# Decay attention and max-MoE on one core: scores of a head as one unit on four lent PSUM banks, and the decays' clip first

## The chip, the cores and the metric

The kernel runs on one core of a Trainium2 chip. The core's engines work side by side, each through its own queue in order: PE (matrix multiply, with PEld for its weight loads), DVE, ACT and POOL (elementwise work and reductions) and SP, which issues the DMAs here. The metric is device time of one execution in microseconds (us), less is better. A measurement of this kernel is the median of a few runs.

## The reference

Decay attention over 8 batches of 8 heads with 576 queries, then a layer of three matrices with a maximum, and an output matrix. All is fp32.

```python
# q, k, v: (8, 8, 576, 64); f: (8, 8, 576); w1, w2, w3: (512, 768); w_out: (768, 512)
scores = scale * np.matmul(q, k.transpose(0, 1, 3, 2))
log_f = np.log(np.clip(f, 0.0001, 1.0))
cum = np.cumsum(log_f, axis=-1)
decay = cum[:, :, :, None] - cum[:, :, None, :]
scores = np.where(causal, -1000000000.0, scores + decay)     # causal: above the diagonal
scores = scores - np.max(scores, axis=-1, keepdims=True)
attn = np.exp(scores)
attn = attn / (np.sum(attn, axis=-1, keepdims=True) + 1e-09)
x = heads side by side of np.matmul(attn, v)                 # (4608, 512)
h = np.maximum(np.maximum(x @ w1, x @ w2), x @ w3)
out = h @ w_out
```

## The kernel before

**Stages.** Heads are numbered n = 0 to 63, eight to a batch. The first batch (n < 8) has a form of its own: q and k come by DMA, PE turns them (`turn_head`, L551), ACT and DVE copy the turned halves out of PSUM (L560, L562), and the matmuls take fp32 operands. From the second batch on (56 heads) scores are made in two passes of faster fp32r matmuls. Pass A (L742) makes the scores with the decay in them. The mask is then added on the diagonal blocks, by PE for n < 16 (L758) and by DVE after that (`cover` L779, `cover_last` L784). ACT and DVE take the maximum over the key blocks (L817, L805, L807, L810), POOL reduces it over the partitions (L820), POOL casts it into a row of the query operand (L823), and pass B (L742 again) adds a term with the negative maximum to the same PSUM columns. ACT takes the exponential out of PSUM (L841). From n = 16 on the sums of the exponentials are made by DVE (L850, L854, L857) and POOL (L865). The values of two heads are multiplied together (`values_pair`, L911), and each batch's result goes through the MoE: `gemm1` (L1071, three matrices) and `gemm2` (L1102, output matrix). The last batch has its own form of the MoE (`moe_last`, L1267).

**Units and banks.** Scores are transposed: keys on the 128 partitions, queries along the columns, five key blocks (the last one 64 keys wide), and only the part on or below the diagonal. A head from the second batch on is two units: unit 2 holds queries 0 to 255 (two matmuls in each pass, of 256 and 128 columns, in bank `sp2`), unit 1 queries 256 to 575 (five matmuls: 320, 320, 192 and 64 columns as one run in banks `sp1/1` and `sp1/0`, and 320 columns as a second run in `sp1/2`). So these four of the eight PSUM banks belong to the scores, and the other four (`mp0` to `mp2`, `t0`) form a pool: a step of `gemm1`, `gemm2` or `values_pair` names a `Slot` in `take=`, gets the bank that came free first, and the step that empties the bank names it in `drop=`. `plan.lend` puts a bank into that pool, the scores' four only at the end, for `moe_last`.

**What sets the order.** Every function only adds steps to `Plan` (engine, cost, keys read and written, priority). `Plan.emit` then lists the steps by a model of the engines: each engine takes, of its steps that are ready, the one with the lowest rank. The rank is the priority, less a share of the length of the chain behind the step, plus a shift drawn at random from `SEEDS` for each four units of priority. Each engine's instructions then stand in that fixed order in its queue, and semaphores hold them at run time.

**The start.** `decay()` loads f by DMA, clips it on DVE (L503), takes the logarithm on ACT (L505), loads the table for the exponential (L507), sums along the row on DVE (L508), and spreads the decays into the key operands (L512 on ACT, L515 and L519 by DMA). Beside it, POOL and DVE clear and fill rows of the operands: POOL writes ones into 64 partitions of each of the eight heads' query operand (L459), constants of the values (L473, L474) and ones for the row sums (L477); DVE writes zeros (L488). 20 matmuls on an identity (L532) fill PE while nothing else is ready.

Of the kernel before, what the change touches and what calls it, by code (L numbers as in the profile page):

```python
# [55 lines left out]
class Plan:  # L56
# [15 lines left out]
    SPAN, WIDTH = 4.0, 0.05  # L72
    STALL = 105.0
    SEEDS = [8126, 4626, 186, 6170, 3404, 2474, 5948, 6407, 9587, 4074, 0, 9657, 1279, 5128, 1368, 6317, 0, 3731, 419]
# [29 lines left out]

    def emit(self):
# [12 lines left out]
        draw = [random.Random(x) for x in self.SEEDS]  # L118

        def shift(prio):  # L120
            w = min(max(int(prio // self.SPAN) + 1, 0), len(draw) - 1)
            return draw[w].gauss(0.0, self.WIDTH) if self.SEEDS[w] else 0.0

        rank = [shift(s[4]) + s[4] - BLW * down[i] / 12000 for i, s in enumerate(self.steps)]
# [123 lines left out]
def kernel(  # L248
# [57 lines left out]
    for c in ("mx", "gm"):  # L306
        plan.parts[c + "1"] = [c + "1a", c + "1b"]
    add = plan.add
# [21 lines left out]
    PW = {1: 3 * S1 + (S - 384) + (S - 512), 2: 384}  # L330
    NQ, Q0 = {1: S1, 2: S2}, {1: S2, 2: 0}
    PF = {u: sb(f"pf{u}", [P, PW[u]]) for u in (1, 2)}
    MX = {u: sb(f"mx{u}", [P, NQ[u]]) for u in (1, 2)}
    GM = {u: sb(f"gm{u}", [P, NQ[u]], F32R) for u in (1, 2)}

    SETS = [("2", MX[2], GM[2], PF[2])]
# [6 lines left out]
    MASKS, WIDE, COPIES = 16, 16, 56  # L343
# [65 lines left out]
    def pb(i, u):  # L409

        return lazy(f"{'pf ph pl'.split()[i]}{u}", [P, PW[u]], F32, "f") if i else PF[u]

# [69 lines left out]
    add("POOL", 1060, sums_constants, ["cs"], [f"rs{g}{u}" for g in range(2) for u in (1, 2)], 0.0, port=1060.0)  # L482
# [3 lines left out]
    for i in range(H):  # L486
        add("POOL", 525, lambda i=i: first_constants(i), w=[f"qf{i}/2"], prio=-9 + i, port=525.0)
        add("DVE", 605, lambda i=i: nc.vector.memset(KF[i][64:P, :], 0.0), w=[f"kf{i}/2"], prio=-5.5 + 0.1 * i)  # L488
    add("POOL", 1650, value_constants, w=[f"vn{i}" for i in range(4)], prio=-8, port=1650.0)


    def decay():

        fx, lx = PF[1][0:BH + 1, 0:S], PF[1][0:BH + 1, S:2 * S]
        ft = fx[0:BH]
        cs = CS
        fs = f.rearrange("b h s -> (b h) s")
# [3 lines left out]
        dma(ft, fs, w=["pf1/0"], prio=DP)  # L501
# [201 lines left out]
    def buffers(n, unit):  # L703
        if n < H * NB32:
            return SETS[n % len(SETS)] if unit == 2 else BUFS[unit]
        return SETS[0] if unit == 2 else BUFS[unit]

# [789 lines left out]
```

## Time and profile before

| | |
|---|---|
| median of 3 runs | 884.13 us (881.48 to 885.15) |
| span of the profiled execution, first to last instruction | 880.1 us |
| median less span (what lies around the span) | 4.0 us |
| PE busy in the span | 868.0 us, 99% |
| DVE, POOL, ACT busy | 680.6, 435.3, 396.8 us |
| mean granted clock of PE | 0.998 |

How to read it: busy time of PE counts a matmul from its start to a modelled end, and matmuls overlap, so busy PE can still hold gaps; the start times of neighbouring matmuls show them. The stages are told apart by a table of busy times for stretches of the span. What an engine waited for is in a list of waits, and the order of single instructions with their starts in the timeline.

### The profile page before, as it was taken

The numbers are of one execution on the slowest core, as the hardware profiler recorded it, in microseconds if no ns is written. First come the engines' busy times: TensorE is split into PE (matmuls) and PEld (weight loads), VectorE is DVE, ScalarE is ACT, GpSimd is POOL, SyncE is SP. The second block draws the span as 40 slices with busy tenths as digits, with TensorE's granted clock in tenths as the row PEclk, the third lists the DMA queues.
The fourth block names the chain that finished last, engine by engine and source line by source line (L and its number), as shares of the span: only waits on it lengthen the run. The fifth ranks groups of instructions, "written<-read, shape, count | busy, mean of one in ns | idle before, by whom it ended". The sixth has DMA issues, their size and how long they took to land.

```text
span 880.1 us, 17952 instructions
## 1 busy us (share of the span) xinstructions
PE 868.0 (99%) x6416; PEld 792.3 (90%) x6416; DVE 680.6 (77%) x1488; ACT 396.8 (45%) x904; POOL 435.3 (49%) x380
## 2 busy tenths in 40 slices
PE   7999999999999999999999999999999999999998
PEld 5989988999989898999989898998989998998997
DVE  7889983678878876877677886787967768798991
ACT  6888553444334434444334443354334434444422
POOL 5655234165666566555474654645564465550000
PEclk9999999999999999999999999999999999999999
DMA  7948456635556455525555354546445444501001
GB/s 204 310 101 274 103 176 165 155 93 143 136 146 154 131 126 143 133 69 150 126 141 147 90 148 102 145 98 168 113 109 156 111 127 101 133 15 39 1 1 61
DMA packets 91834, 110.97 MB, mean 126 GB/s; under 512 B 52461, under 2 KB 54765, under 8 KB 91746
## 3 DMA queue, kind: packets, MB, share of 16 engines
q1 hardware_dynamic: 91746, 109.83, 47.2%
q8 instruction: 51, 0.84, 0.4%
q14 instruction: 37, 0.30, 0.1%
HBM read 50.22 MB, written 9.87 MB: 68 GB/s over the span
## 4 chain that ended last, share of the span: by engine, by line
PE 94%; DVE 3%; ACT 1%; issue 1%; DMA 1%; SPq 0%; DVEq 0%
PE mp L1071 34%; PE s L742 12%; PE t L1071 10%; PE mp L1102 10%; PE mp L911 7%; PE t L1102 5%; PE s L1267 3%; PE mp L1267 2%; PE s L1102 2%; PE t L878 2%; PE t L911 1%; PE t L1267 1%; PE mp L933 1%; DMA sc<-z 1%; PE s L769 0%
## 5 line engine op out<-in xcount | busy, mean ns | idle before, releaser
L1071 PE MATMUL mp<-xh_r,w_r 128*128 128x320 f32 (+1 forms) x1416 | 328.3, 300 | 0.1
L820 POOL PARTITION_ALL_REDUCE gm<-mx x131 | 163.0, 1245 | 206.7 <-DVE mx L810 87.6
L865 POOL PARTITION_ALL_REDUCE z<-va_s x96 | 196.5, 2048 | 136.5 <-DVE va_s L857 69.3
L1071 PEld LDWEIGHTS mp<-xh_r,w_r 128*128 128x128 f32 x1416 | 241.0, 188 | 4.0 <-issue 1.9
L1071 PE MATMUL mp<-xl_r,w_r 128*128 128x320 f32 (+1 forms) x708 | 209.5, 296 | 0.0
L1071 PEld LDWEIGHTS mp<-xl_r,w_r 128*128 128x128 f32 x708 | 133.4, 188 | 0.7
L742 PEld LDWEIGHTS s<-qs_r,ks_r 128*128 128x128 f32 (+1 forms) x784 | 116.6, 181 | 13.7 <-issue 8.1
L742 PE MATMUL s<-qs_r,ks_r 128*128 128x320 f32 (+4 forms) x784 | 128.2, 279 | 0.0
L1071 PE MATMUL t<-xh_r,w_r 128*128 128x320 f32 (+1 forms) x440 | 111.7, 298 | 0.1
L810 DVE TENSOR_TENSOR mx<-mx,s 128x320 f32<-128x320 f32 (+3 forms) x248 | 92.3, 372 | 23.1 <-PE s L742 7.8
L1071 PEld LDWEIGHTS t<-xh_r,w_r 128*128 128x128 f32 x440 | 78.2, 188 | 1.1 <-DVE mx L810 0.5
L1102 PE MATMUL mp<-w_r,hmh_r 128*128 128x512 f32 x228 | 72.9, 401 | 0.0
L1082 DVE TENSOR_TENSOR tm<-mp,tm 128x256 f32<-128x256 f32 (+1 forms) x125 | 56.3, 451 | 16.2 <-PE mp L1071 7.9
L631 DVE STREAM_TRANSPOSE hl<-hl 128x576 f32<-128x576 f32 x56 | 67.8, 1241 | 0.9 <-DMA sc<-z 0.9
L841 ACT ACTIVATE pf<-s 128x512 f32<-128x512 f32 (+4 forms) x107 | 49.6, 506 | 38.2 <-PE s L742 32.8
L1071 PE MATMUL t<-xl_r,w_r 128*128 128x320 f32 (+1 forms) x220 | 65.0, 296 | 0.0
L779 DVE TENSOR_TENSOR s<-s,mask 128x256 f32<-128x256 f32 x96 | 40.8, 426 | 30.2 <-PE s L742 29.9
L1085 ACT ACTIVATE hmh_r<-tm 128x256 fp32r<-128x256 f32 x84 | 34.9, 415 | 59.1 <-DVE tm L1082 58.9
L823 POOL CAST qs_r<-gm 1x256 fp32r<-1x256 f32 (+1 forms) x112 | 56.8, 508 | 7.1
L1080 ACT ACTIVATE tm<-mp 128x256 f32<-128x256 f32 (+1 forms) x66 | 27.1, 410 | 66.4 <-PE mp L1071 58.7
L841 ACT ACTIVATE ph_f<-s 128x384 f32<-128x384 f32 (+2 forms) x80 | 36.8, 505 | 44.4 <-PE s L742 44.4
L817 ACT ACTIVATE mx<-s 128x320 f32<-128x320 f32 (+1 forms) x64 | 26.7, 417 | 64.0 <-DVE s L784 47.8
(418 smaller groups left out, 1754.0 us busy)
## 6 DMA issues: line engine op xcount, KB each, us to landing
qs_r<-hl SPq DMA_DIRECT2D x168, 144.0 KB
ks_r<-hl SPq DMA_DIRECT2D x168, 144.0 KB
w<-in_moe_w_dram SPq DMA_DIRECT2D x9, 1024.0 KB
out_dram<-o_r SPq DMA_DIRECT2D x35, 256.0 KB
hl<-in_k_dram SPq DMA_DIRECT2D x14, 576.0 KB
hl<-in_q_dram SPq DMA_DIRECT2D x14, 576.0 KB
r_r<-rdram SPq DMA_DIRECT2D x56, 144.0 KB
vn<-in_v_dram SPq DMA_DIRECT2D x30, 128.0 KB
```

Of the source, the lines that this page charges most:

```text
L631: add("DVE", 1085, lambda e=e, tt=tt, xs=xs: nc.vector.transpose(tt[:, e], xs[:, e]), [key + "0"], [key + "1"], prio)
L742: nc.tensor.matmul(bank[bk][0:l.shape[-1], col:col + w], l, rhs(qa, w), start=start and bk not in begun, stop=stop, skip_group_check=True)
L810: nc.vector.tensor_tensor(mt[:, a:a + w], mt[:, a:a + w], bank[bk][:, col:col + w], op=ALU.max)
L820: add("POOL", 450 + 2.6 * nq, lambda: nc.gpsimd.partition_all_reduce(gm, mt, P, bass.bass_isa.ReduceOp.max), [km, km + "a"], [kg], prio - ...
L823: add("POOL", 130 + 0.9 * nq, lambda: nc.gpsimd.tensor_copy(QS(s)[96:97, 1, q0:q0 + nq], gm[96:97, :]), [kg], [kx], prio - CB, port=0.6 * ...
L841: add("ACT", act_cost(w), lambda bk=bk, w=w, col=col: nc.scalar.activation(px()[:, col:col + w], bank[bk][:, 0:w], AF.Exp, scale=sc), [kb[ ...
L865: add("POOL", 520 + 5.1 * nq, lambda: nc.gpsimd.partition_all_reduce(Z[:, q0:q0 + nq], blocks_sum()[:, q0:q0 + nq], P, bass.bass_isa.Reduc ...
L911: nc.tensor.matmul(t[D * j:D * j + D, qa:qa + w], vn[:, j, c, 0:D], prs[x][j][0]()[:, col:col + w], start=y == 0, stop=True, skip_group_ch ...
L1071: nc.tensor.matmul(m(), unit_w(i, fb)[:, w, kt, :], xx, start=kt == 0 and x == 0, stop=kt == KT - 1 and x == 2,)
L1082: add("DVE", dve_cost(cn), lambda m=m: nc.vector.tensor_tensor(t, m(), t, op=ALU.max), [km, kt_], [kt_], prio + EV, drop=(slot,))
L1102: nc.tensor.matmul(BANKS[slot.bank][:, 0:cn], l[:, fb, cs], unit_o(fb)[:, r, ds], start=fb == 0 and x == 0, stop=fb == FT - 1 and x == 2,)
L1267: nc.tensor.matmul(bank[c](), w(tw)[:, k], mat(x)[:, tx, k], start=new and k == 0 and z == 0, stop=k == 1 and z == 2, skip_group_check=True)
```

## The change

- From the second batch on, `scores` is called once for a head, with a new unit 0 for all 576 queries. A pass is six matmuls: key block 1 as one of 448 columns where there were 128 and 320, and the other five as before. They stand in two runs, (448, 256) and (320, 320, 192, 64).
- The unit's four banks are no longer its own: each run of pass A takes two `Slot`s, and each of the four exponentials drops one. All eight banks are lent to the pool once the first batch's scores are through.
- With one unit a head has one maximum reduction, one cast and one sum reduction on POOL, of 576 columns. DVE masks the diagonal in four instructions where it had three, and loses the small reduction and copy of unit 2; ACT copies the first block of both ranges of queries (320 and 256 columns). The exponentials stay four.
- The clip of f is added ahead of all other steps, and the clearing and filling steps read its key `clip`, so they stand behind it: on POOL all but the constants, the `less` row and the rows of heads 0 and 1, on DVE those of heads 4 to 7.
- The shift drawn from `SEEDS` is replaced by `MOVES`, a table of some 420 entries: for steps within a range of priority, either every step of one kind moves by a set amount, or all steps by a hashed amount. `MLAG`, the lag of the MoE behind its batch, goes from -0.1 to 1.0 heads.

```diff
-    SEEDS = [8126, 4626, 186, 6170, 3404, 2474, 5948, 6407, 9587, 4074, 0, 9657, 1279, 5128, 1368, 6317, 0, 3731, 419]
+    MOVES = [
+        (56.5, 58.5, 0, 57624, 0.12), (10.7, 11.2, 0, 17111, 0.5), (-20, 100, 1, 54, 0.05),
...
+    def shifts(self):
+
+        kinds, shift = {}, [0.0] * len(self.steps)
+        kind = [kinds.setdefault((s[0], s[2].__code__.co_firstlineno), len(kinds)) for s in self.steps]
+        for low, high, one, x, by in self.MOVES:
+            for i, s in enumerate(self.steps):
+                if low <= s[4] < high and (not one or kind[i] == x):
+                    shift[i] += by if one else by * self.draw(x, i)
+        return shift
...
-        rank = [shift(s[4]) + s[4] - BLW * down[i] / 12000 for i, s in enumerate(self.steps)]
+        rank = [x + s[4] - BLW * down[i] / 12000 for i, (x, s) in enumerate(zip(self.shifts(), self.steps))]
...
+    RUNS, COVER = ((1, 2), (0, 3)), (1, 2, 0, 3)
...
-    add("POOL", 1060, sums_constants, ["cs"], [f"rs{g}{u}" for g in range(2) for u in (1, 2)], 0.0, port=1060.0)
+    fx, lx = PF[1][0:BH + 1, 0:S], PF[1][0:BH + 1, S:2 * S]
+    fs = f.rearrange("b h s -> (b h) s")
+    DP = -10.9
+    dma(fx[0:BH], fs, w=["pf1/0"], prio=DP)
+    dma(fx[BH:BH + 1], fs[1:2], w=["pf1/1"], prio=DP, bytes_=2304)
+    add("DVE", 440, lambda: nc.vector.tensor_scalar(fx, fx, 1e-4, 1.0, op0=ALU.max, op1=ALU.min),
+        ["pf1"], ["pf1", "clip"], DP, port=1.0)
+    add("POOL", 1060, sums_constants, ["cs", "clip"], [f"rs{g}{u}" for g in range(2) for u in (1, 2)], 0.0, port=1060.0)
...
-        add("POOL", 525, lambda i=i: first_constants(i), w=[f"qf{i}/2"], prio=-9 + i, port=525.0)
-        add("DVE", 605, lambda i=i: nc.vector.memset(KF[i][64:P, :], 0.0), w=[f"kf{i}/2"], prio=-5.5 + 0.1 * i)
-    add("POOL", 1650, value_constants, w=[f"vn{i}" for i in range(4)], prio=-8, port=1650.0)
+        add("POOL", 525, lambda i=i: first_constants(i), r=["clip"] if i > 1 else [], w=[f"qf{i}/2"], prio=-9 + i, port=525.0)
+        add("DVE", 605, lambda i=i: nc.vector.memset(KF[i][64:P, :], 0.0), r=["clip"] if i > 3 else [], w=[f"kf{i}/2"], prio=-5.5 + 0.1 * i)
+    add("POOL", 1650, value_constants, r=["clip"], w=[f"vn{i}" for i in range(4)], prio=-8, port=1650.0)
...
+        0: dict(q0=0, nq=S, blocks=[(1, 128, 448, 1, 0), (0, 0, 256, 2, 0), (0, 256, 320, 3, 0), (2, 256, 320, 0, 192),
+                                    (3, 384, 192, 0, 0), (4, 512, 64, 3, 320)], runs=RUNS,
+                exps=[(1, 448, 2, 0), (2, 256, 1, 0), (3, 384, 1, 256), (0, 512, 1, 640)],
+                first=[(256, 320, 3, 0, 1), (0, 256, 2, 0, 1)],
+                more=[(128, 448, 1, 0), (256, 320, 0, 192), (384, 192, 0, 0), (512, 64, 3, 320)]),
...
+        elif unit == 0:
+            slots = [Slot() for _ in range(4)]
+            bank, kb = Lent(slots), [f"sc{n}/{i}" for i in range(4)]
...
             add("PE", ca, lambda run=run: pass_a(run), [kq, kk, "const"], [kb[bk] for bk in run], prio, rows=P,
-                short=0.0 if mask_pe else short[run])
+                short=0.0 if mask_pe else short[run], take=() if first else [slots[bk] for bk in run])
...
+        for bk, w, dst, key in exps:
+            add("ACT", act_cost(w), lambda bk=bk, w=w, dst=dst: nc.scalar.activation(
+                dst(), bank[bk][:, 0:w], AF.Exp, scale=sc), [kb[bk]], key, prio, drop=() if first else (slots[bk],))
...
-    LEAD, MLAG, WP, WR = 2.1, -0.1, 0.7, 0.65
-    DP = -10.9
+    LEAD, MLAG, WP, WR = 2.1, 1.0, 0.7, 0.65
...
-    for key in ("mp0", "mp1", "mp2", "t0"):
+    for key in ("mp0", "mp1", "mp2", "t0", "sp1/0", "sp1/1", "sp1/2", "sp2"):
         plan.lend(key)
...
-        for unit in order:
-            scores(n, unit, p + UP * (unit == 1))
+        scores(n, 0, p + UP)
```

How the change moves instructions, at two places.

DVE at the start of the program, before. `pf` is f, `qs` and `ks` are the operands of heads 0 to 3, `xh` and `xl` those of heads 4 to 7, `u` the decays of the first heads; L488 writes zeros, L503 is the clip, L508 the sum along the row, L515 the decays:

```order
L488 MEMSET qs_65 64x576
L488 MEMSET qs_66 64x576
L488 MEMSET ks_67 64x576
L534 CAST hdl<-ident 128x128
L488 MEMSET ks_68 64x576
L488 MEMSET xh 64x576 x2
L488 MEMSET xl 64x576
L503 TENSOR_SCALAR pf_80<-pf_80 65x576
L488 MEMSET xl 64x576
L508 SCALAR_TENSOR_TENSOR pf_80<-pf_80 65x576
L560 COPY qs_65<-mp_118 64x288
L515 TENSOR_SCALAR u_91<-pf_80 8x576
```

The same place now, where L735 writes zeros, L727 is the clip, L748 the sum along the row, L755 the decays and L800 a copy of a turned operand:

```order
L735 MEMSET ks_67 64x576
L735 MEMSET qs_66 64x576
L735 MEMSET qs_65 64x576
L774 CAST hdl<-ident 128x128
L735 MEMSET ks_68 64x576
L727 TENSOR_SCALAR pf_80<-pf_80 65x576
L735 MEMSET xh 64x576 x2
L748 SCALAR_TENSOR_TENSOR pf_80<-pf_80 65x576
L800 COPY qs_65<-mp_116 64x288
L755 TENSOR_SCALAR u_89<-pf_80 8x576
L800 COPY qs_66<-mp_118 64x288
```

The clip stands ahead of three zero fills that it stood behind, and what hangs on it follows at once.

PE in the middle of the program, before: a whole pass of one head's scores (`s` are the four banks of the scores, `mp` and `t` the pool of four), between `gemm1` matmuls (L1071):

```order
L1071 MATMUL mp_118<-xh_r,w_r 128x320
L742 MATMUL s_114<-qs_r,ks_r 128x320
L742 MATMUL s_113<-qs_r,ks_r 128x320
L742 MATMUL s_113<-qs_r,ks_r 128x192
L742 MATMUL s_114<-qs_r,ks_r 64x64
L742 MATMUL s_115<-qs_r,ks_r 128x320
L742 MATMUL s_116<-qs_r,ks_r 128x256
L742 MATMUL s_116<-qs_r,ks_r 128x128
L1071 MATMUL mp_119<-xh_r,w_r 128x320
```

A whole pass now (L1001; L1329 is `gemm1`):

```order
L1329 MATMUL s_114<-xh_r,w_r 128x256
L1001 MATMUL mp_117<-qs_r,ks_r 128x320
L1001 MATMUL s_111<-qs_r,ks_r 128x320
L1001 MATMUL s_111<-qs_r,ks_r 128x192
L1001 MATMUL mp_117<-qs_r,ks_r 64x64
L1001 MATMUL s_113<-qs_r,ks_r 128x448
L1001 MATMUL s_112<-qs_r,ks_r 128x256
L1329 MATMUL s_114<-xh_r,w_r 128x256
```

The last matmul of 128 columns is gone into one of 448; one of the head's banks is here a `mp` bank, and the scores' former banks serve `gemm1`.

## Rows read from the trace of the kernel before

**Rows 1.** The page, part 1: busy us (share of span) and instructions

```profile
PE 868.0 (99%) x6416; PEld 792.3 (90%) x6416; DVE 680.6 (77%) x1488; ACT 396.8 (45%) x904; POOL 435.3 (49%) x380
```

**Rows 2.** Busy times by stretch of the span, its columns first

```profile
core 0: us, PE busy (x) PEld busy (x) DVE busy (x) ACT busy (x) POOL busy (x), PEclk, DMA share, GB/s
0.00:22.00 22.00, 16.54 (x103) 11.29 (x104) 15.94 (x30) 13.43 (x28) 11.69 (x31) 0.92 0.73 204
22.00:44.00 22.00, 22.00 (x174) 20.90 (x174) 18.20 (x33) 17.80 (x41) 14.48 (x14) 1.00 0.92 310
44.00:88.00 44.00, 40.59 (x332) 38.66 (x330) 40.05 (x70) 37.77 (x75) 22.89 (x20) 1.00 0.65 188
...
110.00:770.00 660.00, 659.85 (x4902) 600.28 (x4902) 500.99 (x1133) 274.15 (x646) 366.57 (x302) 1.00 0.51 131
...
860.00:880.00 20.00, 17.06 (x91) 14.35 (x90) 0.43 (x2) 3.17 (x6) 0.00 (x0) 1.00 0.18 67
```

**Rows 3.** The list of what PE waited for: us, times, longest

```profile
PE mp L551 <- ACT qs L562: 3.5, 1, 3.5
PE mp L878 <- ACT hmh L841: 1.7, 1, 1.7
```

**Rows 4.** Timeline of the start, all engines: start us, us, engine, line, operation

```profile
2.94 0.25 POOL L473 MEMSET vn<- 64x130 f32 x1
...
5.34 1.09 POOL L459 MEMSET ks<- 64x576 f32 x2
...
5.62 3.22 DVE L503 TENSOR_SCALAR pf<-pf 65x576 f32<-65x576 f32 x1
...
7.43 1.09 POOL L459 MEMSET xl<- 64x576 f32 x2
...
8.87 0.68 ACT L505 ACTIVATE pf<-pf 65x576 f32<-65x576 f32 x1 [6.64 <-DVE pf L503]
...
9.59 1.35 DVE L508 TENSOR_TENSOR_SCAN pf<-pf 65x576 f32<-65x576 f32 x1
...
11.21 0.44 DVE L515 TENSOR_SCALAR u<-pf 8x576 f32<-8x576 f32 x1
...
11.83 1.37 ACT L512 ACTIVATE qs<-pf 1x576 f32<-1x576 f32 x2
...
11.86 0.74 PE L551 MATMUL mp<-hdl,w 96*128 96x96 f32 x3 [3.50 <-ACT qs L562]
...
15.00 0.64 PE L742 MATMUL s<-qs 128*128 128x160 f32 x4
```

**Rows 5.** The clip's line: DVE's queue at the semaphore of f's DMA

```profile
L503 DVEq EVENT_SEMAPHORE  x1: 21/21/21, 4.1 to 4.1; - x1
```

**Rows 6.** Timeline of PE around one pass of unit 2

```profile
258.15 0.34 PE L742 MATMUL s<-qs_r,ks_r 128*128 128x256 f32 x2
258.32 0.33 PE L1071 MATMUL t<-xh_r,w_r 128*128 128x256 f32 x1
258.49 0.28 PE L1071 MATMUL t<-xl_r,w_r 128*128 128x256 f32 x1
258.61 0.41 PE L1071 MATMUL t<-xh_r,w_r 128*128 128x256 f32 x2
258.86 0.28 PE L1071 MATMUL t<-xl_r,w_r 128*128 128x256 f32 x1
```

**Rows 7.** Groups by line and shape: count, then busy us and mean ns

```profile
L742 PE MATMUL s<-qs_r,ks_r 128*128 128x128 f32 x112 | 25.0, 223 | 0.0
```

**Rows 8.** The same view, other engines, work that the change replaces

```profile
L820 POOL PARTITION_ALL_REDUCE gm<-mx x131 | 163.0, 1245 | 206.7 <-DVE mx L810 87.6 <-DVE mx L807 69.6 <-DVE sc L1034 13.9
...
L807 DVE TENSOR_REDUCE mx<-s 128x128 f32<-128x256 f32 x59 | 24.5, 415 | 0.8 <-ACT mx L817 0.4
...
L841 ACT ACTIVATE ph_f<-s 128x384 f32<-128x384 f32 x40 | 19.7, 491 | 31.1 <-PE s L742 31.1
...
L805 DVE COPY mx<-s 128x128 f32<-128x128 f32 x51 | 14.5, 284 | 10.6 <-PE s L758 8.2 <-ACT mx L817 0.9
```

More of the change, by code (lines that the diff above doesn't have):

```diff
@@ L103, in add, with draw @@
         self.steps.append((eng, cost, fn, deps, prio, xfer, rows, short, light, take, drop, port, late, more))
+    @staticmethod
+    def draw(seed, i):
+        x = (i * 0x9E3779B1 + seed * 0x85EBCA77) & 0xFFFFFFFF
+        for turn, times in ((15, 0x2C1B3C6D), (12, 0x297A2D39), (15, 1)):
+            x = ((x ^ (x >> turn)) * times) & 0xFFFFFFFF
+        return x / 2147483648.0 - 1.0
+    def shifts(self):
[6 more added lines that the diff above has]
+        return shift
     def emit(self):
@@ L794, in scores, with cover_one @@
             add("PE", ca, lambda run=run: pass_a(run), [kq, kk, "const"], [kb[bk] for bk in run], prio, rows=P,
-                short=0.0 if mask_pe else short[run])
+                short=0.0 if mask_pe else short[run], take=() if first else [slots[bk] for bk in run])
         if not mask_pe:
-            add("DVE", 335, cover, ["const"], [kb[0]], prio)
-            if unit == 1:
-                add("DVE", 135, cover_last, ["const"], [kb[1]], prio)
+            def cover_one(bk):
+                nc.vector.tensor_tensor(bank[bk][:, 0:P], bank[bk][:, 0:P], mask, op=ALU.add)
+            for bk in COVER:
+                if bk == 0:
+                    add("DVE", 335, cover, ["const"], [kb[0]], prio)
+                elif bk == 3:
+                    add("DVE", 135, cover_last, ["const"], [kb[3]], prio)
+                else:
+                    add("DVE", 202, lambda bk=bk: cover_one(bk), ["const"], [kb[bk]], prio)
         def most():
@@ L835, in scores @@
                 [kb[bk] for bk in run], prio, rows=P, short=0.0 if first else short[run])
-        for bk, w, col in d["exps"]:
-            if first:
-                key = PFKEYS.get((unit, bk), [f"pf{name}"])
-            else:
-                key = [f"{pk}/{bk}"] if unit == 1 else [pk]
-            add("ACT", act_cost(w), lambda bk=bk, w=w, col=col: nc.scalar.activation(
-                px()[:, col:col + w], bank[bk][:, 0:w], AF.Exp, scale=sc), [kb[bk]], key, prio)
+        for bk, w, dst, key in exps:
+            add("ACT", act_cost(w), lambda bk=bk, w=w, dst=dst: nc.scalar.activation(
+                dst(), bank[bk][:, 0:w], AF.Exp, scale=sc), [kb[bk]], key, prio, drop=() if first else (slots[bk],))
         if n < WIDE:
@@ L922, in values_pair @@
                 half, z0 = nq // 2, nq
-                runs = [[(max(qa, half * a), min(qa + w, half * a + half), col - qa) for c, qa, w, col in cols] for a in range(2)]
+                runs = [[(max(qa, half * a), min(qa + w, half * a + half), v, col - qa) for c, qa, w, v, col in cols] for a in range(2)]
                 runs = [[x for x in xs if x[0] < x[1]] for xs in runs]
@@ L1378 @@
     QP = -0.3
-    UO = 1
     LO = -2.55
@@ L1457 @@
             if b == B - 1:
-                for i in range(3):
-                    plan.lend(f"sp1/{i}")
-                plan.lend("sp2")
                 moe_last(b, lambda x, n=n: n + 1 + MLAG + H * x)
```

110 lines of the change are left out of this document (52 added, 58 removed), and 224 rows, old and new, of the table MOVES.

## The prediction

> **What bounds the kernel now.** I read the busy times first: PE is busy 868.0 of 880.1 us, DVE 77%, POOL 49%, ACT 45% [rows 1]. By stretches, PE has no idle time from 22 to 44 us and 0.15 us in the 660 us from 110 to 770, at full clock; it idles 5.5 us in the first 22 us, 3.4 us from 44 to 88, and 2.9 us in the last 20, behind the last output [rows 2]. So in nearly the whole span a microsecond is won only by giving PE less to do, and only at the start by letting it begin earlier. The list of waits names two large ones: 3.5 us for ACT's copies of turned operands (L562), at the start, and 1.7 us for an exponential of the first batch [rows 3]. The timeline of the start says what ACT was late for [rows 4], and the timeline of PE shows what a busy PE hides: the distance of the starts of neighbouring matmuls [rows 6].
>
> **Part 1, the scores' matmuls.** A pass loses its matmul of 128 columns; the columns go into one of 448, so their own streaming time stays. What goes is a gap. Unit 2's two matmuls start at 258.15, the next matmul 0.17 us later, and this one, of 256 columns, keeps PE for 0.17 us until the next start. The matmuls of the same 256 columns after it take 0.12 us each (258.49 to 258.61, and two from 258.61 to 258.86) [rows 6]. So the 128-column matmul leaves 0.05 us of waiting behind it; I read it as too short to cover the load of the weights after it. The change has 112 of them, two passes of 56 heads [rows 7]: 112 x 0.05 = 5.6 us. The rows are rounded to 0.01 us, so 0.04 to 0.06, 4.5 to 6.7 us. The run that ends in 64 columns stays, and with it its own gap. All of this lies where PE is the bound, so it counts in full.
>
> Here the Trainium skill can be weighed. Its page "TensorE: Matmul & The Clock Gate", section "Back-to-back issue gap", gives the distance of two matmuls as N/2.4 + 2.5 ns when warm; by that alone 112 matmuls fewer with the same columns save an estimated 0.3 us. The same page's section "LDWEIGHTS (loading the stationary operand)" has 128 columns of weights take P/1.2, 107 ns, which a matmul of 128 columns (an estimated 56 ns by the first formula) would not cover, leaving an estimated 51 ns. Row and second rule agree; the row decides.
>
> **Part 2, the clip.** The load of f was through at 4.1 us [rows 5]. The clip stood behind DVE's zero fills and began at 5.62, and then took 3.22 us, where another scalar operation over 576 columns, L515, took 0.44. In that time POOL ran its fills of ones one behind the other, from 5.34 to 8.52; the clip ended at 8.84, right behind them [rows 4]. So it waited for POOL. Behind it waited ACT's logarithm, 6.64 us, and behind that in ACT's queue every copy of turned operands, for which PE waited 3.5 us [rows 3, 4]. Now three fills fewer stand ahead of the clip on DVE, and POOL's long fills stand behind it: 4.1 + 0.44 = 4.55 instead of 8.84, 4.3 us earlier. That is the upper end.
>
> The lower end comes from the fills that moved. They run from 4.55 on, beside what follows the clip. The values' constants and the fills took from 2.94 to 8.52, 5.6 us, so POOL is at them until about 10.1. In that stretch DVE reaches L515's successor (L755), due at 4.55 + (11.21 - 8.84) = 6.9. If it waits for the end of the fills, as the clip did, it ends at 10.5; queued behind it on DVE is the copy of head 1's turned query (0.4 us), for which ACT's next copy from that bank and then PE's next turn wait. ACT would be ready for it at 13.20 - 4.3 = 8.9 (the end of L512 [rows 4], moved up). So up to 10.9 - 8.9 = 2.0 us are given back, and 2.3 remain. I take 3.3, the middle, as the rows hold one case of each kind: a clip that waited for the whole chain, and an L515 that met none. POOL's first maximum finds its fills done well before it, and the DMA queue's order hardly matters here, since the first heads' loads still stand in front.
>
> The Trainium skill's page "SBUF — State Buffer", section "SBUF: two separate sides", has POOL and DVE share one port pair as a lock that is held for a whole instruction. By it the clip should have got in after one fill, an estimated 0.6 us, and not after six; L755 would then hold things up by no more than that, and this part would be an estimated 3.7 to 4.3. The trace shows the longer wait, so 3.3 stands.
>
> From there on PE has work without a pause from 22 to 44 us and for all but 3.4 us from 44 to 88 [rows 2], so a start 3.3 us earlier should arrive at the end.
>
> **Part 3, what lies beside PE.** A head loses a DVE reduction of 0.415 and a copy of 0.284 us, and one of POOL's two maximum reductions of 1.245 on average [rows 8]; DVE gains a mask instruction and 128 columns of a maximum, ACT a copy of 256 columns. That is less for DVE and POOL and up to 0.5 us a head more for ACT (below its exponential of 384 columns, 0.491 [rows 8]), 28 us on an engine that is busy 45%. I count it at nothing: PE waits for none of them from 110 to 770. The cover is PE's other work. If it were gone, the chain from pass A to pass B would show: POOL's reduction over 576 columns instead of 256 or 320 is at most twice as long, 1.2 us more a head. The order leaves room for that: a block's pass B now stands at least 43 matmuls behind its pass A, where it was 20 (the 256 columns of unit 2) or 25 (unit 1); at 0.12 us each [rows 6] 5.2 us instead of 2.4 and 3.0. The new table and the later MoE get no term. They only reorder, and there is next to no idle time to win beyond 88 us; what they may lose is the rivals'. The 2.9 us at the end are the last output's and stay.
>
> **The sum.** 880.1 - 5.6 - 3.3 = 871.2 for the span. The median of the runs is 4.0 above the profiled span, so 884.1 - 8.9 = 875.2 us. The bounds of both parts (4.5 to 6.7 and 2.3 to 4.3) give 873.1 to 877.3.
>
> **Rivals.**
> - *The start is not handed on.* From 22 to 44 us the DMA engines are 92% busy, and from 44 to 88 DVE has 40.1 of 44 us of work and ACT 37.8 [rows 2]: one of them, not PE, may set the pace of the first batch, and the weights for the MoE may come no earlier. Against it: PE has no idle in the first of these stretches, and DVE itself is rid of 2.8 us of a stuck clip. Then only part 1 counts: 884.1 - 5.6 = 878.5.
> - *The scores gain nothing.* Either the gap does not hang on the short matmul and stays in the pass at another place, or it goes and PE waits the same 0.1 us a head (5.6 / 56) elsewhere, since banks are now taken just as they come free. The first of the two rules above comes out here: it knows no such gap. For it: the gap is a matter of 0.05 us, read from one place. Against: the 64-column run stays as it is, and 448 and 256 columns are both longer than any matmul here needs to cover a load. Then 884.1 - 3.3 = 880.8.
> - *Slower: the lent banks.* A head's four banks come back one by one, each behind an exponential of about 0.49 us on ACT [rows 8], and up to two heads can hold all eight. If PE reaches a matmul that takes such a bank one exponential too early for each of 56 heads, that is 56 x 0.49 = 27 us, less 8.9: 902. It decides from 8.9 / 56 = 0.16 us a head. Against it: the MoE's matmuls and the values already live on four banks taken in just this way, and PE idles 0.15 us in 660 [rows 2]; with eight in the pool there is not less to choose from.
>
> **How the numbers follow.** The forecast has 0.67, the start that is not handed on 0.12, the scores that gain nothing 0.14, the slower case 0.07. The forecast's own range, with what reordering may cost or give, is 871 to 879.5. For 8 in 10 the range takes in the first rival and nearly all of the second: 870 to 881. A measurement of this kernel tells about 0.5% from no change, 4.4 us: below 879.7 or above 888.5. Faster takes the forecast and most of the first rival, 0.77; the second rival and the edges are the same, 0.17; slower 0.06, the third where it costs more than 13 us.
>
> **What would show it.** In the changed kernel's profile: a clip of about 0.4 us that starts near 4.1; the logarithm near 4.6 instead of 8.87; first scores near 11.7 instead of 15.00; no wait of 3.5 us at the turned operands; whether L755 takes 0.4 us or some 3. Matmuls of 448 and 256 columns with no gap behind them, six score matmuls in a pass where there were seven, PE idle still near nothing from 110 to 770. The forecast is wrong if PE's list of waits shows exponentials or POOL's casts again and again in the middle of the span (third rival), if PE's busy time there isn't shorter although the matmuls are fewer (second), or if the idle time of PE between 44 and 88 grows by what the start won (first).

## The result, and the profile after

The changed kernel takes 875.84 us (median of 4 runs, 875.25 to 875.90), the kernel before 884.17 in the runs beside it: a ratio of 0.9908, with a 95% interval of 0.9893 to 0.9923. That is 8.3 us less, where 8.9 was forecast. The profiled execution took 875.77 us with a span of 874.0.

The page's first part of the changed kernel, to be held against [rows 1]:

```profile
PE 863.2 (99%) x6304; PEld 783.5 (90%) x6304; DVE 652.0 (75%) x1384; ACT 401.7 (46%) x952; POOL 376.8 (43%) x220
```

PE has 112 matmuls fewer and 4.8 us less busy time; DVE and POOL have less to do, as the diff says. Busy times by stretch (columns as in [rows 2]):

```profile
0.00:22.00 22.00, 19.49 (x122) 13.99 (x123) 17.43 (x35) 16.30 (x36) 13.03 (x32) 1.00 0.77 228
...
44.00:88.00 44.00, 41.37 (x327) 38.29 (x326) 37.80 (x66) 39.17 (x80) 19.05 (x14) 1.00 0.72 224
...
110.00:770.00 660.00, 657.47 (x4819) 594.02 (x4816) 475.80 (x1036) 280.79 (x694) 311.98 (x150) 1.00 0.51 129
```

In the first 22 us PE is busy 3 us more than in [rows 2], and its clock is 1.00 there instead of 0.92. In the middle, though, where PE idled 0.15 us, it now idles 2.5. From 44 to 88 us it idles 2.6 us, where it was 3.4: what the start won is not lost there. The list of what PE waited for:

```profile
PE s L1329 <- DVE tm L1340: 1.6, 2, 1.0
PE mp L1217 <- ACT ph L1151: 0.8, 1, 0.8
...
PE t L1001 <- POOL qs_r L1088: 0.6, 1, 0.6
```

The 3.5 us at the turned operands [rows 3] are gone; the first and the third row are new, and both lie in the middle. The timeline of the start, to be held against [rows 4]:

```profile
3.36 0.28 POOL L713 MEMSET vn<- 64x130 f32 x1
...
4.35 0.48 DVE L727 TENSOR_SCALAR pf<-pf 65x576 f32<-65x576 f32 x1
...
4.87 0.68 ACT L745 ACTIVATE pf<-pf 65x576 f32<-65x576 f32 x1 [2.63 <-DVE pf L727]
...
7.47 1.09 POOL L699 MEMSET xl<- 64x576 f32 x2
...
7.93 0.94 DVE L755 TENSOR_SCALAR u<-pf 8x576 f32<-8x576 f32 x1
...
11.73 0.84 PE L1001 MATMUL s<-qs 128*128 128x256 f32 x4
```

The clip (L727) takes 0.48 us, the logarithm (L745) starts 4.0 us earlier, and the first scores (L1001) come 3.3 us earlier in this execution. The decays (L755) took 0.94 us: they got through behind the second of the two fills beside them, which ended at 8.56. The key `clip` only orders the planner's list: on the chip POOL does not wait for the clip, its constants (L713) begin at 3.36, before it, and its fills run from 5.38 to 8.56. And one pass of a head's scores on PE, for [rows 6]:

```profile
219.03 0.36 PE L1001 MATMUL s<-qs_r,ks_r 128*128 128x448 f32 x1
219.23 0.28 PE L1001 MATMUL mp<-qs_r,ks_r 128*128 128x256 f32 x1
219.34 0.31 PE L1001 MATMUL s<-qs_r,ks_r 128*128 128x320 f32 x1
...
219.72 0.19 PE L1001 MATMUL s<-qs_r,ks_r 128*64 128x64 f32 x1
219.75 0.39 PE L1329 MATMUL s<-xh_r,w_r 128*128 128x320 f32 x1
219.99 0.31 PE L1329 MATMUL s<-xl_r,w_r 128*128 128x320 f32 x1
```

From start to start 448 columns keep PE 0.20 us and 256 keep it 0.11, no more than elsewhere: no gap is left there. Behind the 64 columns it is still seen: the 320 columns at 219.75 hold PE for 0.24 us, where 320 take 0.15 (219.34 to the next start at 219.49).

### The profile page after: what moved, and what is told of

The parts are those of the page before. It is cut to its first block, busy times and chain, and to the rows that moved or that the text cites. A ratio compares the mean times of both kernels' runs of the same rounds, so it can differ in the third digit from the quotient of the medians.

```text
span 874.0 us, 17381 instructions
## 1 busy us (share of the span) xinstructions
PE 863.2 (99%) x6304; PEld 783.5 (90%) x6304; DVE 652.0 (75%) x1384; ACT 401.7 (46%) x952; POOL 376.8 (43%) x220
## 4 chain that ended last, share of the span: by engine, by line
PE 85%; DVE 4%; POOL 1%; issue 1%; DMA 1%; ACT 1%; SPq 1%; DVEq 0%; POOLq 0%
PE s L1329 22%; PE mp L1329 16%; PE s L1360 8%; PE mp L1360 6%; PE t L1329 5%; PE s L1001 5%; PE mp L1001 4%; PE mp L1170 3%; PE s L1170 3%; PE s L1525 3%; PE t L1360 3%; PE mp L1525 2%; PE t L1170 2%; PE t L1001 1%; DVE mx L1075 1%
## 5 line engine op out<-in xcount | busy, mean ns | idle before, releaser
L1329 PE MATMUL s<-xh_r,w_r 128*128 128x320 f32 (+1 forms) x960 | 229.3, 301 | 1.6 <-DVE tm L1340 1.6
L1329 PEld LDWEIGHTS s<-xh_r,w_r 128*128 128x128 f32 x960 | 165.3, 188 | 6.8 <-issue 3.7
L1329 PE MATMUL mp<-xh_r,w_r 128*128 128x256 f32 (+1 forms) x688 | 164.0, 298 | 0.2 <-DVE tm L1340 0.2
L1329 PE MATMUL s<-xl_r,w_r 128*128 128x320 f32 (+1 forms) x480 | 142.4, 297 | 0.0
L1329 PEld LDWEIGHTS mp<-xh_r,w_r 128*128 128x128 f32 x688 | 118.8, 188 | 5.2 <-issue 3.7
L1329 PE MATMUL mp<-xl_r,w_r 128*128 128x320 f32 (+1 forms) x344 | 101.4, 295 | 0.0
L1329 PEld LDWEIGHTS s<-xl_r,w_r 128*128 128x128 f32 x480 | 90.4, 188 | 0.5
L1001 PE MATMUL s<-qs_r,ks_r 128*128 128x320 f32 (+4 forms) x320 | 70.6, 290 | 0.0
L1001 PE MATMUL mp<-qs_r,ks_r 128*128 128x320 f32 (+4 forms) x268 | 65.5, 292 | 0.0
L1329 PEld LDWEIGHTS mp<-xl_r,w_r 128*128 128x128 f32 x344 | 64.8, 188 | 0.3
L1340 DVE TENSOR_TENSOR tm<-s,tm 128x320 f32<-128x320 f32 (+1 forms) x90 | 40.2, 451 | 30.0 <-PE s L1329 17.2
L1329 PE MATMUL t<-xh_r,w_r 128*128 128x320 f32 (+1 forms) x224 | 55.7, 301 | 0.0
L1001 PEld LDWEIGHTS s<-qs_r,ks_r 128*128 128x128 f32 (+1 forms) x320 | 52.5, 182 | 2.3 <-issue 0.5
L1001 PEld LDWEIGHTS mp<-qs_r,ks_r 128*128 128x128 f32 (+1 forms) x268 | 44.1, 177 | 2.5 <-issue 0.7
L1088 POOL CAST qs_r<-gm 1x576 fp32r<-1x576 f32 x56 | 44.4, 793 | 3.6
```

Source lines behind the costliest of these rows:

```text
L1001: nc.tensor.matmul(bank[bk][0:l.shape[-1], col:col + w], l, rhs(qa, w), start=start and bk not in begun, stop=stop, skip_group_check=True)
L1088: add("POOL", 130 + 0.9 * nq, lambda: nc.gpsimd.tensor_copy(QS(s)[96:97, 1, q0:q0 + nq], gm[96:97, :]), [kg], [kx], prio - CB, port=0.6 * ...
L1329: nc.tensor.matmul(m(), unit_w(i, fb)[:, w, kt, :], xx, start=kt == 0 and x == 0, stop=kt == KT - 1 and x == 2,)
L1340: add("DVE", dve_cost(cn), lambda m=m: nc.vector.tensor_tensor(t, m(), t, op=ALU.max), [km, kt_], [kt_], prio + EV, drop=(slot,))
```

## The experiments

In most kernels below the planned order of the steps and the choice of banks are written out as a fixed list (of either kernel), so that one edit changes one thing; otherwise the planner, given one step more, would put all of them in another order. Ratios are against the kernel before, run on the same chip between the kernel's own runs. The kernel before was at 882.2 to 883.6 us there; 0.001 of it is 0.9 us. A difference of two ratios is uncertain by about 0.002, or 1.8 us.

### The changed kernel again

Only `emit` differs: it goes through the list.

> The changed kernel once more, with its planned order of steps and its choice of banks written out as a fixed list, so that the next kernels can differ from it by one edit alone. Every theory expects the time of the changed kernel, 875.8 us, within 1 us, and a span 1.8 us below it.

875.29 us (6 runs, 873.41 to 875.98), ratio 0.9912 (0.9895 to 0.9928). What lies around the span is 1.8 us in each run. In its profile PE idles 1.1 us from 110 to 770, and of the three waits in the middle only the one of 1.0 us is there; the others come and go. The start of the scores comes and goes as well:

```profile
13.19 0.85 PE L1001 MATMUL s<-qs 128*128 128x256 f32 x4
```

The order is the same and the execution no slower (875.41 us), the logarithm begins at 4.85, and yet the first scores are 1.5 us later than the 11.73 above. So one profile's first scores don't measure what a start is worth; the clip and the logarithm are steadier. This is the base for the next ones.

### The 128 columns back, last in the run

```diff
-blocks=[(1, 128, 448, 1, 0), (0, 0, 256, 2, 0), ...
+blocks=[(1, 256, 320, 1, 128), (0, 0, 256, 2, 0), (1, 128, 128, 1, 0), ...
```

> The changed kernel in its fixed order, with the matmul of 448 columns split into 320 and 128 again, and the one of 128 columns last in its run, where it stood before the change; 112 more matmuls, the same columns. Theory (the short matmul leaves about 0.05 us behind it, because the load of the next weights lasts longer than it does): 112 x 0.05 = 5.6 us more, 881.4 us, with a bound of 880.3 to 882.5. Rival (the scores gained nothing, and the change's gain beyond the start came from the new order): the time of the changed kernel and at most 0.3 us more, below 876.5 us.

880.23 us (12 runs), ratio 0.9971 (0.9960 to 0.9982): 0.0059 or 5.2 us above the changed kernel. The 112 matmuls cost what the theory says, 0.046 us each, though their columns are the same.

### The 128 columns back, between longer matmuls

```diff
-blocks=[(1, 128, 448, 1, 0), (0, 0, 256, 2, 0), ...
+blocks=[(1, 128, 128, 1, 0), (1, 256, 320, 1, 128), (0, 0, 256, 2, 0), ...
```

> The changed kernel in its fixed order, with the matmul of 448 columns split as 128 and 320, the one of 128 columns now first in its run and between longer matmuls of the same scores, where the kernel before had it last. Theory (the gap hangs on the short matmul and the next load of weights, wherever it stands): the same loss as with the 128 columns last, which was 0.0059 of the time of the kernel before, 4.4 to 5.8 us over the changed kernel. Rival (the gap hangs on the end of a run, where PE goes from scores to other work): the time of the changed kernel and at most 0.3 us more.

881.62 us (12 runs), ratio 0.9986 (0.9975 to 0.9997): 6.5 us above, more than the 4.4 to 5.8 expected, but not by more than the 1.8 that such a difference is uncertain by. So the gap goes with the short matmul and not with the end of a run. PE's timeline of this kernel has it inside the pass:

```profile
220.52 0.42 PE L1001 MATMUL s<-qs_r,ks_r 128*128 128x128 f32 x2
220.78 0.28 PE L1001 MATMUL mp<-qs_r,ks_r 128*128 128x256 f32 x1
```

The 128 and the 320 columns behind them (one row, "x2") hold PE for 0.26 us, where 448 in one hold it for 0.20.

The traces also say what the gap is. From 110 to 770 us the start of the next matmul follows 0.117 us after one of 256 columns, 0.147 after 320, 0.20 after 448 and 0.232 after 512 (medians), so a column costs about 0.455 ns and a matmul as such nothing. After 128 columns it follows 0.060 us later, but the 320 columns behind them then take 0.20. And two loads of 128x128 weights (f32 in the rows) never start less than 0.107 us apart, in 3620 to 3726 pairs in each of four traces (before, changed, and the two with the 128 columns back). A matmul of 0.060 us thus leaves 0.047 to its next load, 112 x 0.047 = 5.3 us.

### The kernel before, with the clip first

```diff
 L488 MEMSET ks_68 64x576
+L503 TENSOR_SCALAR pf_80<-pf_80 65x576
 L488 MEMSET xh 64x576 x2
-L488 MEMSET xl 64x576
-L503 TENSOR_SCALAR pf_80<-pf_80 65x576
-L488 MEMSET xl 64x576
+L488 MEMSET xl 64x576 x2
```

> The kernel before, in its own order written out as a fixed list, with one edit: the clip stands ahead of DVE's last four zero fills. The second part of the change alone. Theory (the prediction's part 2): the clip takes about 0.5 us from 4.1 on, the logarithm begins near 4.9, PE's 3.5 us wait at the turned operands goes, and the time is 3.3 us less than that of the kernel before (2.3 to 4.3), 879.2 us where its median was 882.5. Rival (what the start wins is not handed on, as the kernel with the clip moved back suggests): first scores some 3 us earlier, and the time within 1 us of 882.5.

878.72 us (6 runs), ratio 0.9946 (0.9929 to 0.9964): 4.8 us less (3.2 to 6.3), where the theory had 3.3 (2.3 to 4.3). The rival falls: what the start wins does arrive. The timeline of this kernel's DVE, where the decays (L515) are stuck for 1.41 us beside one long fill of POOL, and then PE in two of its stretches (columns: stretch, length, PE busy, clock, DMA share, GB/s):

```profile
4.21 0.46 DVE L503 TENSOR_SCALAR pf<-pf 65x576 f32<-65x576 f32 x1 [0.45 <-DMA pf<-in_f_dram]
...
8.85 1.41 DVE L515 TENSOR_SCALAR u<-pf 8x576 f32<-8x576 f32 x1
```

```profile
8.00:12.00 4.00, 4.00 (x19) 1.00 1.03 264
12.00:16.00 4.00, 4.00 (x40) 1.00 0.64 118
```

The same two stretches of the kernel before:

```profile
8.00:12.00 4.00, 0.50 (x3) 0.95 1.01 268
12.00:16.00 4.00, 4.00 (x23) 0.63 0.49 92
```

PE's long wait from 8 to 12 us was followed by a lower granted clock: a mean of 0.63 over 4 us, between the levels of 1.2 and 2.4 GHz. In this profile the early clip takes away the wait and, with it, this loss of (1 - 0.63) x 4 = 1.5 us of full clock.

### The kernel before again

> The kernel before, its order written out as a fixed list and nothing else changed. The question is whether its clip is stuck in every execution. Theory (the order of the fills decides): the clip takes about 3.2 us again, the logarithm begins near 8.9, and the granted clock from 12 to 16 us is 0.6 to 0.7 again. Rival (it is chance who gets in): the clip takes 0.5 to 1.6 us, and the logarithm begins before 7.5. Every theory expects the median of the kernel before, 882.5 us, within 1 us.

882.28 us (12 runs), ratio 0.9991 (0.9979 to 1.0004). The clip is stuck again, for 3.21 us, so it is not the chance of one execution:

```profile
5.61 3.21 DVE L503 TENSOR_SCALAR pf<-pf 65x576 f32<-65x576 f32 x1
```

But in this execution the clock fell at another place, behind PE's wait for the first batch's exponentials:

```profile
56.00:60.00 4.00, 2.33 (x11) 0.79 0.63 143
60.00:64.00 4.00, 4.00 (x28) 0.79 0.72 157
```

Runs list their mean clock, and the 75 of the kernel before sort by it: 13 at 1.000 with a median of 881.2 us, 30 at 0.998 with 882.2, 27 at 0.996 with 883.9, 4 at 0.994 with 884.7, and one at 0.997. So 0.002 of the mean go with 0.8 to 1.7 us, where 880 x 0.002 would be 1.8 us of full clock. That is most of the spread of the kernel before, 880.7 to 885.6. With the clip first five of six runs are at 1.000, and of the changed kernel's ten (the first four and its repetition) eight.

### The changed kernel, with the clip behind the zero fills

```diff
 L735 MEMSET ks_68 64x576
-L727 TENSOR_SCALAR pf_80<-pf_80 65x576
 L735 MEMSET xh 64x576 x2
+L735 MEMSET xl 64x576
+L727 TENSOR_SCALAR pf_80<-pf_80 65x576
```

> The changed kernel in its fixed order, with the clip put back behind three more of DVE's zero fills, as it stood before the change; POOL's order is unchanged. Theory (the clip is then beside POOL's unbroken fills again and waits for their end, near 8.6 us; what the start wins arrives at the end): the clip takes 2 to 3 us and not 0.48, the first scores come about 3 us later, and the time is 3.3 us more, 879.1 us (878.1 to 880.1). Rival (the start is not handed on): first scores later, but 875.8 us. Rival (POOL is no part of it): the clip takes 0.5 us, ends near 6.7 us, and the time is at most 1.9 us more.

875.38 us (6 runs), ratio 0.9917 (0.9901 to 0.9932): no difference. The clip was late, but was not stuck:

```profile
5.70 0.57 POOL L699 MEMSET xh<- 64x576 f32 x1
...
6.05 0.53 DVE L727 TENSOR_SCALAR pf<-pf 65x576 f32<-65x576 f32 x1
...
12.30 0.89 PE L1001 MATMUL s<-qs 128*128 128x256 f32 x4
```

It came 1.7 us later than in the changed kernel and was through half a us after its start. The logarithm began at 6.62, 1.8 us late, and the first scores came between those of the two profiles of the changed kernel (11.73 and 13.19). In time it is 0.4 us, uncertain by 2.0. My theory that it would wait for the end of the fills falls, and the numbers are those of the second rival, a clip that POOL does not hold. Whether so small a delay is handed on can't be told from this run; the next one delays the start by more.

### The changed kernel, with the clip made to wait

As the last one, with POOL's last fill awaited:

```diff
+nc.vector.tensor_copy(TM[0][0:1, 1:2], QF[6][64:65, 0:1])
 nc.vector.tensor_scalar(fx, fx, 1e-4, 1.0, op0=ALU.max, op1=ALU.min)
```

> The changed kernel in its fixed order, with the clip behind DVE's three zero fills and, through a copy of one element that POOL's last fill writes, behind POOL's fills as well: the clip then ends near 9 us, as it did before the change, whatever the engines do to each other. Theory (what the start loses arrives at the end): the logarithm begins near 9, PE waits about 3 us for turned operands, the granted clock falls behind that wait as it did before the change (0.63 from 12 to 16 us), the first scores come near 15 us, and the time is 3.3 us more than 875.3 us, 878.6 (877.6 to 879.6). Rival (the start is not handed on): first scores near 15 us all the same, and the time within 1 us of 875.3.

879.91 us (11 runs), ratio 0.9966 (0.9953 to 0.9979): 4.8 us above the changed kernel. The timeline of its start:

```profile
8.41 1.06 POOL L717 MEMSET ph<- 97x1152 f32 x1
...
8.56 1.22 DVE L727 TENSOR_SCALAR pf<-pf 65x576 f32<-65x576 f32 x1
...
9.81 0.68 ACT L745 ACTIVATE pf<-pf 65x576 f32<-65x576 f32 x1 [7.58 <-DVE pf L727]
...
16.14 0.92 PE L1001 MATMUL s<-qs 128*128 128x256 f32 x4
```

The clip ended at 9.78 and not near 9, and the logarithm began 4.9 to 5.0 us later than in the two profiles of the changed kernel (4.87 and 4.85): 4.8 us arrive, so this start is handed on about one to one. That is more than the expected 3.3, for a later clip than the kernel before has (8.84). The first scores are 4.4 us later than in the one profile and 3.0 than in the other. In the profiled run the clock stayed at 1.00, against the theory; of the eleven runs two were at 1.000 and nine at 0.994 to 0.998. Here the clock doesn't sort the times: the two at 1.000 took 879.81 and 880.58 us, so the 4.8 us are waiting.

### POOL's fills beside the early clip

```diff
 L699 MEMSET qs_66 64x576
+L699 MEMSET ks_67 64x576
+L699 MEMSET xh 64x576 x2
+L699 MEMSET ks_68 64x576
+L699 MEMSET xl 64x576
 L713 MEMSET vn_75 64x2x65
```

> The changed kernel in its fixed order, with one edit on POOL: five of its fills of ones (0.54 us each) stand ahead of the values' constants, so that the clip, which is early, meets them. Theory (the prediction's reading of the clip before the change: it waits for the end of an unbroken row of POOL's fills): it begins near 4.3 and ends with the fills, near 6.5, so it takes about 2.2 us; the time is at most 2 us more, 875.3 to 877.3. Rival (it waits for the one fill that is running): the clip takes less than 1.1 us and the time is the changed kernel's, 875.3. The Trainium skill's page SBUF — State Buffer, section SBUF: two separate sides, states a lock on the port that POOL and DVE share, held for a whole instruction; by it the rival is right.

874.11 us (6 runs, 873.04 to 876.96), ratio 0.9900 (0.9881 to 0.9919). The rival is right: the clip got in behind one fill, and the pair of fills took 1.40 us instead of 1.09 to let it by.

```profile
3.95 1.40 POOL L699 MEMSET xh<- 64x576 f32 x2
4.23 0.60 DVE L727 TENSOR_SCALAR pf<-pf 65x576 f32<-65x576 f32 x1
...
10.58 0.89 PE L1001 MATMUL s<-qs 128*128 128x256 f32 x4
```

It is the lowest median of all, with first scores earlier than in both profiles of the changed kernel (11.73 and 13.19); the intervals don't tell it from that one.

### The fills in the order of the kernel before

The clip behind the zero fills as above, and POOL's fills as two of keys and two pairs.

> The changed kernel in its fixed order, with the clip behind three of DVE's zero fills as in the run with the clip moved back, and POOL's six fills of ones in the order that the kernel before has (two of keys, then the two pairs), where the changed kernel has one of keys, a pair, one of keys, a pair. Theory (which fills follow each other decides whether DVE's clip gets in between them): the clip is stuck for some 3 us again, to the end of the fills. Rival (its phase against the fills decides, not their order): it gets in behind one or two of them, in less than 1.2 us.

One run, 876.11 us:

```profile
6.06 0.53 DVE L727 TENSOR_SCALAR pf<-pf 65x576 f32<-65x576 f32 x1
```

The clip took 0.53 us, with the fills in the order of the kernel before: that order alone is not what holds it.

### The waits in the middle taken away

The wait of 1.0 us is in each profile of the changed kernel. Its rows there, DVE, POOL and PE:

```profile
361.21 3.59 POOL L1124 PARTITION_ALL_REDUCE z<-va_s  x1 [5.27 <-ACT mx L1082]
...
361.97 1.80 DVE L1292 TENSOR_SCALAR sc<-sc 64x18 f32<-64x18 f32 x1
...
366.92 0.48 DVE L1340 TENSOR_TENSOR tm<-s,tm 128x320 f32<-128x320 f32 x1
...
367.46 0.42 PE L1329 MATMUL s<-xh_r,w_r 128*128 128x320 f32 x1 [1.01 <-DVE tm L1340]
```

A tiny operation of the row sums (L1292) is stuck 1.80 us beside POOL's sum reduction, so DVE comes late to L1340, which empties PE's next bank. The edit at this place (two more are alike):

```diff
-L1292 TENSOR_SCALAR sc<-sc 64x18
 L1037 TENSOR_TENSOR mp_118<-mp_118,mask 128x2x128
-L1293 RECIPROCAL sc<-sc 64x18
 L871 STREAM_TRANSPOSE hl<-hl 128x18x32
+L1340 TENSOR_TENSOR tm_109<-s_114,tm_109 128x320
 L1075 TENSOR_TENSOR mx<-mx,mp_117 128x448
 ...
-L1340 TENSOR_TENSOR tm_109<-s_114,tm_109 128x320
+L1292 TENSOR_SCALAR sc<-sc 64x18
+L1293 RECIPROCAL sc<-sc 64x18
```

> The changed kernel in its fixed order, with some DVE steps swapped at the three places in the middle of the span where PE waits (0.63, 1.01 and 0.65 us): the maximum that empties PE's next bank goes ahead of the head's transposes and score maxima at two places, the small operations of the row sums go behind them at the second, and at the third two subtractions go behind the maximum, so that POOL's cast does not meet a chain of them. Theory (these waits are DVE's order and nothing else): all three waits go, 2.3 us less, 873.5 us. Rival (a wait that is taken away comes back at the next bank or the next cast): within 0.5 us of the changed kernel, 875.8 us, with other waits of the same sum in PE's list.

876.42 us (6 runs), ratio 0.9925 (0.9907 to 0.9943): nothing won. PE idles 2.6 us from 110 to 770. The rival is right, and the profile of this kernel has the place:

```profile
367.27 0.16 DVE L1292 TENSOR_SCALAR sc<-sc 64x18 f32<-64x18 f32 x1
...
367.52 3.23 POOL L1085 PARTITION_ALL_REDUCE gm<-mx  x1 [1.86 <-DVE sc L1292]
367.65 1.29 DVE L877 SCALAR_TENSOR_TENSOR hl<-hl 128x1152 fp32r<-128x1152 f32 x1
...
371.73 0.96 PE L1001 MATMUL mp<-qs_r,ks_r 128*128 128x320 f32 x5 [1.35 <-POOL qs_r L1088]
```

L1292 takes 0.16 us now. But DVE's next long operation (L877) runs beside POOL's maximum, which takes 3.23 us instead of 1.96, and PE waits 1.35 us for the cast behind it. In the first profile of the changed kernel the two met in the same way, POOL at 367.17 and L877 at 367.32, and there it was L877 that took longer, 2.21 us.

### The orders straight from the planner

The changed kernel with `MOVES = []`, and the kernel before with `SEEDS = [0] * 19`.

> The changed kernel with the table MOVES empty, so that the planner orders the steps by priority and chain alone; one unit a head, lent banks and the early clip stay. Theory (the prediction's part 3: the table only reorders and is worth next to nothing): within 2 us of the changed kernel, and PE idle less than 4 us from 110 to 770. Rival (lent banks cost much, and the table is what hides it, the prediction's slower rival): waits of PE for exponentials and casts all through the middle, 0.1 to 0.2 us a head and more, 881 us or above.

> The kernel before with all its SEEDS zero, so that the planner orders its steps by priority and chain alone, as in the run of the changed kernel without its table. It tells whose cost the changed kernel's table hides. Theory (lent banks and one unit a head are what needs a tuned order; with banks of its own the old form is less sensitive): less than 8 us above the kernel before, below 891 us, and PE idle less than 4 us from 110 to 770. Rival (any order straight from the planner costs that much here): 15 to 25 us above it, 898 to 908 us, with waits for exponentials and casts as in the changed kernel without its table.

900.02 us (4 runs), ratio 1.0204 (1.0187 to 1.0221), and 895.91 us (4 runs), ratio 1.0147 (1.0123 to 1.0170). The theory of the first falls: the table is worth 25 us. The bound of the second falls as well: the old form too loses 13 to 14 without its shifts, between the theory's 8 and the rival's 15. So about half of the 25 us is the price of any order straight from the planner, and the rest is the changed form's own (units, lent banks, and a lag of the MoE that was set together with the table). PE's busy time from 110 to 770 us in the one and in the other:

```profile
110.00:770.00 660.00, 651.11 (x4744) 585.41 (x4743) 480.15 (x1014) 277.92 (x681) 303.07 (x147) 1.00 0.50 129
```

```profile
110.00:770.00 660.00, 651.51 (x4819) 590.63 (x4818) 494.09 (x1107) 269.11 (x638) 357.42 (x296) 0.99 0.50 129
```

8.9 and 8.5 us idle: in the middle, lent banks show no more of it in sum than banks of the scores' own. Over the whole span PE idles 26.0 us without the table and 10.8 with it; the other 9.7 us are PE's busy time, 872.9 against 863.2 for the same 6304 matmuls, of which the mean clock of 0.994 would make about 5 (0.006 x 899). The largest waits of PE in the changed kernel without its table are single ones, the first of them in the last batch's MoE:

```profile
PE mp L1525 <- ACT ph_st L1417: 4.8, 1, 4.8
PE s L1001 <- POOL qs_r L1088: 2.2, 1, 2.2
PE mp L1001 <- POOL qs_r L1088: 2.1, 2, 1.5
PE s L1001 <- ACT pf L1109: 1.8, 5, 0.9
```

But those for POOL's casts (L1088), 6.0 us in four waits, all lie in the middle, and the list of the old form without its shifts has none of that kind there.

## Why the prediction came out

**Part 1 was right**, in cause and size: 5.6 us (4.5 to 6.7) were forecast, and putting the short matmul back costs 5.2 at one place and 6.5 at another. That a short matmul waits for the next load was a reading of one place; the distances of the loads, 0.107 us and more, now bear it out. The Trainium skill (page "TensorE: Matmul & The Clock Gate", section "Back-to-back issue gap") gives the formula behind the 0.3 us for an isolated matmul and says itself that it under-counts at small N, where the load is left out; so it never was a rival to the rule on the load (same page, section "LDWEIGHTS (loading the stationary operand)"), whose 107 ns the traces agree with.

**Part 2 was right in that the late clip holds up the start; its size was probably too small.** Forecast were 3.3 us (2.3 to 4.3). The kernel before with the clip first is 4.8 us (3.2 to 6.3) faster than the kernel before beside it, and 4.0 faster than that kernel's repetition from a fixed list. What was left out is the clock. At a mean clock of 1.000 alone, the kernel before has 881.2 us (13 runs) and the one with the early clip 878.2 (five): 3.0 us, about the waiting that the sum priced; the other 1 to 1.8 us go with the clock that falls behind PE's waits. [rows 2] had it, as a 0.92 in the first 22 us, and I read past it. The late clip in the changed kernel is no second measure of this term: it ended 5.0 us later than in the changed kernel, while in the kernel before it ended 4.0 later.

The lower end did not come about, but its working failed at another step than it names: the fills were taken to run from 4.55 to 10.1, behind the clip, and they ran to 8.56, as POOL does not wait for the clip. L755 was due at 6.9 and came at 7.93; it was held to the end of these fills and took 0.94 us. Elsewhere it took 0.44 to 1.41, never held up for longer than one POOL instruction takes. Why the clip of the kernel before is held by a whole row of fills stays open (see the end). The first rival, a start that is not handed on, is refuted by the early clip in the kernel before and the late one in the changed kernel.

**Part 3's zero did not hold.** PE idles 1.1 to 2.6 us from 110 to 770 in the nine profiles of the changed form in a fixed or tuned order, and 0.15 to 0.40 in the three of the old one. The step that failed is "I count it at nothing: PE waits for none of them": DVE, late beside POOL, does make PE wait. The times agree, but weakly. The two kernels that have the early clip and the short matmul, the changed one (0.9971) and the kernel before (0.9946), differ by 0.0025, 2.2 us, uncertain by 0.0021. It is the same 2.2 us by which parts 1 and 2, 5.2 and 4.8, are more than the 7.8 won (0.9912). What is beyond the idle time stays open.

**"They only reorder" failed in a larger way.** No term was given to the table because there was no idle time to win. But the table is part of what keeps it so: without it the change is at 900 us, where the third rival had its 902, and without either search the changed form is slower than the old one (1.0204 against 1.0147), despite 10 us of less work and earlier start. The mechanism of that rival, one exponential a head, isn't what is seen there; single long waits are, in the middle those for POOL's casts, and busy time that is longer for the same matmuls. Which of the changes makes the new form need its table more is not shown.

**The base** was off by a term as well: 4.0 us were put around the span, from the median of some runs and the span of another. It is 1.7 to 1.9 in every run; the profiled execution, at a mean clock of 0.998, was one of the faster ones. The sum was taken off the median, so this did no harm. That the forecast of 875.2 came out so near 875.84 is in part luck: part 2's missing 0.7 to 1.5 us and part 3's 1 to 2 nearly cancel.

**What would show it**: the clip came at 4.35 us with 0.48, the logarithm at 4.87 (4.6 forecast), the first scores at 11.73 (11.7, but the repetition has 13.19, so this match is luck), six matmuls without a gap in a pass; only the idle time from 110 to 770, forecast as near nothing, did not hold.

## What to carry to other kernels

A matmul too short to cover the next load of weights costs the same wherever it stands; on a PE that is full, merging its columns into a longer one is worth the count times the gap. A wait of PE is worth more than its length where the granted clock falls behind it, so read the clock of the stretch after each wait, and sort the runs by their clock before explaining a spread. And a form that looks neutral on engines with time to spare has to be judged with an order searched for it: here the order was worth more than the change.

## What was not expected of the hardware

- **A row of fills that lets nobody in, in one kernel only.** In the kernel before the clip waited 3.21 and 3.22 us through five joints between POOL's fills; in three others it got in at the next joint (0.53, 0.60, 0.53). It came at the same point of a fill, 0.28 us after its start, in the kernel before (5.33 and 5.61) and in the one with the fills beside the early clip (3.95 and 4.23). The Trainium skill (page "SBUF — State Buffer", section "SBUF: two separate sides") has a lock for one whole instruction: that holds in the three, and for 1.22 us behind a single fill of 1.06 us; in the kernel before it does not. Nor does it for L755 in the changed kernel, which began at 7.93, while the fill that began at 7.99 went first. Neither the order of the fills, nor the clip's place on DVE, nor its point within a fill explains it alone, and it stays open.
- **It goes both ways.** POOL's cast, 0.79 us in the mean, took 2.53 beside two of DVE's subtractions in the changed kernel's profile:

```profile
383.23 2.53 POOL L1088 CAST qs_r<-gm 1x576 fp32r<-1x576 f32 x1
...
383.82 1.41 DVE L1310 TENSOR_TENSOR xl_r<-u,xh_r 128x576 fp32r<-128x576 f32 x2
```

- **The clock falls behind one wait and not behind its like.** From 56 to 60 us PE is busy 2.33 of 4 us in one profile of the kernel before, with a clock of 0.79, and 2.31 of 4 in the other, with 1.00. Which executions fall is not settled by these runs; nor is why falls are rarer with the early clip. They are not gone: the profile of the kernel with the waits in the middle taken away has the early clip (4.31 us) and a fall at the start, where PE was busy 2.64 us from 4 to 8:

```profile
8.00:12.00 4.00, 3.95 (x14) 0.57 0.97 270
```
